# Rebalancing the first eleven slots of a top-k attention with a GELU layer behind it: normalisations to Pool, one addition and one copy later in their queues

## The chip, the cores and the metric

The kernel runs on one core of one Trainium2 chip. A core has five engines that each work through their own program in order and wait for each other by semaphores: TensorE (PE, with its weight loads shown apart as PEld), VectorE (DVE), ScalarE (ACT), GpSimd (Pool) and SyncE (SP), which here only issues transfers. The metric is the device time of one execution in microseconds. Before the change it is 1646.02 us, the median of three runs (1644.73 to 1646.81).

## The reference: what is computed

The inputs q, k and v are 8 batches x 8 heads x 576 rows x 64, and w_in (512 x 2048) and w_out (2048 x 512). For every row of scores the 32 largest are kept, and the softmax runs over them; then a two-layer block with the exact GELU follows.

```python
scores = scale * np.matmul(q, k.transpose(0, 1, 3, 2))
kth = np.partition(scores, -top_k, axis=-1)[..., -top_k:-top_k + 1]     # top_k = 32
scores = np.where(scores >= kth, scores, -1000000000.0)
scores = scores - np.max(scores, axis=-1, keepdims=True)
attn = np.exp(scores)
attn = attn / (np.sum(attn, axis=-1, keepdims=True) + 1e-09)
attn_out = np.matmul(attn, v)
x = attn_out.transpose(0, 2, 1, 3).reshape(B * S, H * D)                # 4608 x 512
h = x @ w_in
out = (0.5 * h * (1.0 + erf(h / sqrt(2)))) @ w_out
```

The two weights reach the kernel as 64-bit floats, seen as integers. The kernel turns them into 32-bit floats itself, with integer steps on their words: two ScalarE activations on the exponent part, a scaling of the low word ("conversion"), and two integer additions on Pool ("first sum" and "second sum").

## The kernel before

The work is cut into items: two heads of one batch by 128 rows of scores (the last 64 rows of two pairs of heads form one item). A loop over slots n keeps several items in flight: slot n computes the scores of item n+2, finds the 32 largest of item n (VectorE), runs the softmax of item n-1 (ScalarE), transposes the normalised item n-2 (TensorE, copied out of PSUM by ScalarE), multiplies a finished pair of items with v ("attend", item n-3), and fills TensorE with pieces of the two-layer block (`mlp`). The 16 units of the weights are converted in slots 1 to 15 and 17, one a slot. START is 10: the slot from which pieces of the two-layer block are there to do.

```python
def weights_size(u):                        # ScalarE, at the end of slot n-1 for the unit of slot n
    ...
    nc.scalar.activation(d, first, func=AF.Relu, bias=low, scale=2.0**19)
    nc.scalar.activation(below, first, func=AF.Prelu, bias=high, scale=2.0**-21, alpha=2.0**40)
    if not on_pool(u):                                                   # conversion, L179
        nc.scalar.activation(w.bitcast(i32), w.bitcast(u32), func=AF.Copy, scale=2.0**-13)

def on_pool(u):
    return SLOT_OF[u] >= START

def weights_add(u):                         # Pool, at the start of slot n
    if u in words:
        w, _, below, d = parts(u)
        if on_pool(u):                                                   # conversion, L191
            nc.gpsimd.tensor_scalar(w.bitcast(i32), w.bitcast(u32), 2.0**-13, None, op0=ALU.mult)
        nc.gpsimd.tensor_tensor(d, d, below, op=ALU.add)                 # first sum, L194
        nc.gpsimd.tensor_tensor(d, d, w.bitcast(i32), op=ALU.add)        # second sum, L195
    made.add(u)
...
def threshold(i):                           # Pool: neg (L345), bias (L348) for the softmax of item i
...
def inverse(i):                             # VectorE, L356
    nc.vector.reciprocal(st["rden"], st["den"])

def add_small(i):                           # Pool, L362
    nc.gpsimd.tensor_scalar(st["den"], st["den"], 1e-9, None, op0=ALU.add)

def softmax(i, e):                          # ScalarE, L369 and L370
    nc.scalar.activation(s, s, func=AF.Prelu, bias=st["neg"][:, e, 1:2], scale=1.0, alpha=STEEP)
    nc.scalar.activation(s, s, func=AF.Exp, bias=st["bias"][:, e : e + 1], scale=1.0,
                         accum_out=st["den"][:, e : e + 1])

def normalise(i, on_dve):                   # L382: on_dve of the two rows on VectorE, the others on Pool
    for e in range(2):
        s = row(i, e)
        (nc.vector if e >= 2 - on_dve else nc.gpsimd).tensor_scalar(
            s, s, st["rden"][:, e : e + 1], None, op0=ALU.mult)
...
# attend: 20 matmuls into o (L450), then
            nc.scalar.copy(out=xT[:, at, c], in_=o[:, 0:n])              # L455
...
# transposes: tails (matmul L401, copy L402), then main(0) and main(1) (matmuls L419, copies L426)
...
for n in range(ahead):
    left[0] = 4 if n in (START, START + 1) else 8
    eager[0] = n > N
    weights_add(unit_in(n))
    scores(n + 2)                           # matmuls L273, L277; copies L287, L288 on ScalarE
    product = attend(n - 3)
    late = n > START
    mlp(1)
    tr = transposes(n - 2)
    ...
    softmax(n - 1, 0)
    mlp(1)
    if not late:
        softmax(n - 1, 1)
    ...                                     # transposes of item n-2, pieces of q and k, mlp
    if late:
        softmax(n - 1, 1)
    add_small(n - 1)
    ...
    if n < N:
        top_k(n, {3: lambda: inverse(n - 1)})   # 8 maxima and 6 replacements on VectorE, then the reciprocal
    else:
        inverse(n - 1)
    threshold(n)
    u = unit_in(n + 1)
    normalise(n - 1, 0 if u not in words else 2 if on_pool(u) else 1)
    weights_size(unit_in(n + 1))
    if n >= FIRST:
        load_weights(n + 2)                 # into a staging place that the unit of slot n has left
```

tp_t, tp, t_ps, o and tp_qk share one pair of PSUM buffers.

Of the kernel before, what the change touches and what calls it, by code (L numbers as in the profile page):

```python
# [14 lines left out]
def kernel(  # L15
# [19 lines left out]
    nc = tc.nc  # L35
# [32 lines left out]
    xT = const.tile([P, KO, RING], f32, name="xT")  # L68
# [12 lines left out]
    def raw_of(n, pair):  # L81
        return raws[n][pair % len(raws[n])]

    def load(n, pair, queue=None, queue2=None):
        if pair >= n_pairs:
            return
        queue = queue or nc.sync
        queue2 = queue2 or queue
        b, h0 = pair // NP, 2 * (pair % NP)
        t, src = raw_of(n, pair), sources[n]  # L90
        for e in range(2):
            queue.dma_start(
                out=t[:, 0:NM, e, :], in_=src[b, h0 + e, 0:SM].rearrange("(t p) d -> p t d", p=P)
            )
            queue2.dma_start(out=t[e * TL : (e + 1) * TL, NM, e, :], in_=src[b, h0 + e, SM:S])
# [18 lines left out]
    def weights_of(u):  # L114

        if u < NWI:
            c, r = u // 2 * WS, u % 2 * 2
            return w_in, r, c, w_in_sb[:, r : r + 2, c : c + WS]
        r = 2 * (u - NWI)
        return w_out, r, 0, w_out_sb[:, r : r + 2, :]  # L120
# [4 lines left out]
    START = 2 * NP + 2  # L125
    WARM = 9
    words = {}
# [6 lines left out]
    SLOT_OF = {u: FIRST + i + (i == UNITS - 1) for i, u in enumerate(ORDER)}  # L134
    UNIT_IN = {n: u for u, n in SLOT_OF.items()}
    unit_in = UNIT_IN.get
# [29 lines left out]
    def parts(u):  # L166

        t, dst = words[u], weights_of(u)[3].bitcast(i32)
        return t[:, :, 0::2], t.bitcast(mybir.dt.int16)[:, :, 2::4], t[:, :, 1::2].bitcast(i32), dst
# [10 lines left out]

    def on_pool(u):

        return SLOT_OF[u] >= START

    made = set()

    def weights_add(u):
        if u in words:
            w, _, below, d = parts(u)
            if on_pool(u):  # L190
                nc.gpsimd.tensor_scalar(  # L191
                    w.bitcast(i32), w.bitcast(u32), 2.0**-13, None, op0=ALU.mult
                )
            nc.gpsimd.tensor_tensor(d, d, below, op=ALU.add)  # L194
            nc.gpsimd.tensor_tensor(d, d, w.bitcast(i32), op=ALU.add)  # L195
        made.add(u)


    items, starts = [], []
# [8 lines left out]
    def place_of(b, row):  # L208

        if row < SM:  # L210
            return b // 2 * RING + b % 2 * (SM + 2 * TL) + row
        return b // 2 * RING + SM + b % 2 * TL + row - SM
# [34 lines left out]
    def row(i, e):  # L247
        return S_of[i][:, e * S : (e + 1) * S]
# [5 lines left out]
    def half(r, e):  # L254


        return slice((r ^ e) * TL, ((r ^ e) + 1) * TL)
# [100 lines left out]
    def add_small(i):  # L358
        if i < 0 or i >= N:
            return  # L360
        st = stat_of[i]
        nc.gpsimd.tensor_scalar(st["den"], st["den"], 1e-9, None, op0=ALU.add)  # L362

    def softmax(i, e):

        if i < 0 or i >= N:
            return
        st, s = stat_of[i], row(i, e)
        nc.scalar.activation(s, s, func=AF.Prelu, bias=st["neg"][:, e, 1:2], scale=1.0, alpha=STEEP)  # L369
        nc.scalar.activation(  # L370
            s, s, func=AF.Exp, bias=st["bias"][:, e : e + 1], scale=1.0,
            accum_out=st["den"][:, e : e + 1],
        )

    def normalise(i, on_dve):

        if i < 0 or i >= N:
            return
        st = stat_of[i]
# [3 lines that stand above are left out]
                s, s, st["rden"][:, e : e + 1], None, op0=ALU.mult  # L383
            )
# [5 lines left out]
    def transposes(i):  # L390
# [24 lines left out]
        def main(e):  # L415
            tp = ps.tile([P, 512], f32, tag="tp", name="tp")
            first = e * (S + TL if t < NM else S)
            for j in range(NM):
                nc.tensor.transpose(  # L419
                    tp[:, j * P : (j + 1) * P], s[:, first + j * P : first + (j + 1) * P], ident  # L420
                )
            if t < NM:
                dst = pt_now[0][:, e * NM : (e + 1) * NM, t % 2 * P : (t % 2 + 1) * P]
            else:
                dst = ptt[:, e, 0:NM, :]
            nc.scalar.copy(out=dst, in_=tp.rearrange("p (j n) -> p j n", j=NM))  # L426

        return [tails] + [lambda e=e: main(e) for e in range(2)]

    n_tok, read = [0], [0]  # L430

    def attend(i):

        if i < 0 or i >= N:
            return False
        pair, t = items[i]
        b, at = divmod(pair, NP)
        if t < NM and t % 2 == 0:
            return False
        pt = pt_now[0]  # L440
        o = ps.tile([P, 512], f32, tag="tp", name="o")
        n, row = (2 * P, (t - 1) * P) if t < NM else (TL, SM)
        tok = place_of(b, row)
        assert read[0] >= tok + n - RING
        c = slice(tok % RING, tok % RING + n)
        if t < NM:
            vt = raw_of("v", pair)
            for j in range(NJ):
                for e in range(2):
                    nc.tensor.matmul(  # L450
                        o[e * D : (e + 1) * D, 0:n], lhsT=vt[:, j, e, :],
                        rhs=pt[:, e * NM + j if j < NM else 2 * NM, :],
                        start=(j == 0), stop=(j == NJ - 1),
                    )
            nc.scalar.copy(out=xT[:, at, c], in_=o[:, 0:n])  # L455
        else:
            for r in range(2):
                vt = raw_of("v", pair + r)
                for j in range(NJ):
                    for e in range(2):  # L460
                        nc.tensor.matmul(  # L461
                            o[e * D : (e + 1) * D, r * TL : (r + 1) * TL], lhsT=vt[:, j, e, :],
                            rhs=pt[:, r, j, half(r, e)], start=(j == 0), stop=(j == NJ - 1),
                        )
            nc.scalar.copy(
                out=xT[:, at : at + 2, c],
                in_=o[:, 0 : 2 * TL].rearrange("p (r n) -> p r n", r=2),
            )

        if t == (NM if b % 2 == 0 else NM - 1):  # L470
            for r in range(2 if t == NM else 1):
                load("v", pair + r + NP + 1)
        if at == (NP - 1 if t < NM else NP - 2):
            assert n_tok[0] == tok
            n_tok[0] = tok + n
        return True
# [111 lines left out]
    def mlp(n):  # L588
        for _ in range(n):
            if done[0] >= len(pieces) or pieces[done[0]][0] > ready[0] or left[0] == 0:  # L590
                return
            pieces[done[0]][1]()
            done[0] += 1
            left[0] -= 1
            if eager[0]:
                run_gelus()
# [38 lines left out]
# [5 lines that stand above are left out]
        scores(n + 2)  # L640
        product = attend(n - 3)
        late = n > START
        mlp(1)
        tr = transposes(n - 2)
        if product and n > START and done[0] < len(pieces) and pieces[done[0]][0] > ready[0]:

            for piece in tr[:1]:
                piece()
            tr, ready[0] = tr[1:], n_tok[0]
        softmax(n - 1, 0)  # L650
        mlp(1)
        if not late:
            softmax(n - 1, 1)
        mlp(1)
        prep = prep_in.pop(n, [])
        if len(prep) > 1 and len(tr) == 3:
            tr, prep = tr[:1] + prep[:1] + tr[1:], prep[1:]
        for piece in tr[:-1]:
            piece()
            ready[0] = n_tok[0]  # L660
            mlp(1)
        ready[0] = n_tok[0]
        if late:
            softmax(n - 1, 1)
        add_small(n - 1)
        for piece in tr[-1:] + prep:
            piece()
            mlp(1)

        run_gelus()  # L670
        mlp(left[0])
        run_gelus()
        if n < N:
            top_k(n, {3: lambda: inverse(n - 1)})
        else:
            inverse(n - 1)
        threshold(n)
        u = unit_in(n + 1)

        normalise(n - 1, 0 if u not in words else 2 if on_pool(u) else 1)  # L680

        weights_size(unit_in(n + 1))
        if n >= FIRST:
            load_weights(n + 2)
        if n <= NP:
            load("v", n)
# [38 lines left out]
```

## Time and profile before

The span of the profiled execution is 1643.7 us.

| engine | busy us | share of the span |
|---|---|---|
| TensorE, matmuls | 1589.8 | 97% |
| VectorE | 1421.2 | 86% |
| ScalarE | 1184.8 | 72% |
| Pool | 650.3 | 40% |

The operations that the change touches, with the mean time of one (in the first 150 us):

| line | engine | operation | ns |
|---|---|---|---|
| L382 | VectorE | normalisation, 128x576 | 520 |
| L382 | Pool | normalisation, 128x576 | 1729 |
| L194, L195 | Pool | first and second sum, 128x1024 | 2400, 2397 |
| L191 | Pool | conversion, 128x1024 | 3108 |
| L179 | ScalarE | conversion, 128x1024 | 1138 |
| L455 | ScalarE | copy to xT, 128x256 | 377 |

A page of the profile gives the busy time of each engine, a picture of the span in forty slices (about 41 us each, digits are tenths busy), and groups of instructions by line of the kernel. The trace behind it can be asked for the instructions of one engine in order of time, for who waited for whom, and for the busy time in chosen stretches. Times in these answers count from the start of the span. In a timeline a line reads: start, duration, engine, line, operation, output<-input, shape; the brackets hold the idle time of the engine just before it and what ended it. An average over the span mixes stages with different limits, so each stage has to be looked at by itself.

### The profile page before, as it was taken

How to read it: one execution, taken by the hardware profiler on the slowest of the kernel's cores; microseconds unless marked ns; L12 is line 12 of the kernel's file. 1: busy time of each engine (PE TensorE's matmuls, PEld its weight loads, DVE VectorE, ACT ScalarE, POOL GpSimd, SP SyncE). 2: the span in 40 equal slices, each digit the busy share in tenths (PEclk: the TensorE clock that was granted, in tenths of full speed). 3: DMA queues.
4: the chain of work that ended last, by engine and by line, in shares of the span. 5: the costliest groups of instructions: out<-in, count | busy, mean ns of one | idle time of the engine just before them, and what ended most of it. 6: DMA issues, size and time to landing. Idle time of an engine off the chain costs nothing.

```text
span 1643.7 us, 25039 instructions
## 1 busy us (share of the span) xinstructions
PE 1589.8 (97%) x8818; PEld 1076.9 (66%) x8818; DVE 1421.2 (86%) x3058; ACT 1184.8 (72%) x2131; POOL 650.3 (40%) x749
## 2 busy tenths in 40 slices
PE   6669999999999999999999999999999999999999
PEld 4346676766666666676666667676666666667665
DVE  7999999988899889998989888998889898999800
ACT  6889877777777777777777777777777777777620
POOL 3778633333333333333333333333333333333300
PEclk7779999999999999999999999999999999999999
DMA  6424210011101110011110111001110101000000
GB/s 179 141 86 132 55 43 1 14 29 43 37 1 29 30 34 24 1 28 36 29 28 9 34 30 43 1 14 29 44 36 1 28 16 35 2 14 1 7 13 13
DMA packets 126765, 56.14 MB, mean 34 GB/s; under 512 B 117776, under 2 KB 118064, under 8 KB 126640
## 3 DMA queue, kind: packets, MB, share of 16 engines
q1 hardware_dynamic: 125376, 54.12, 12.3%
q8 instruction: 70, 1.15, 0.3%
q14 instruction: 55, 0.45, 0.1%
q10 hardware_dynamic: 1200, 0.39, 0.1%
q0 software_dynamic: 64, 0.03, 0.0%
HBM read 45.08 MB, written 9.44 MB: 33 GB/s over the span
## 4 chain that ended last, share of the span: by engine, by line
PE 92%; DVE 6%; ACT 1%; POOL 1%; issue 0%; DVEq 0%; POOLq 0%; ACTq 0%
PE h_ps L502 31%; PE y_ps L538 30%; PE o L450 9%; PE s_ps L277 8%; PE tp L419 7%; DVE top L330 3%; DVE rest L333 2%; PE tp_qk L232 2%; PE t_ps L273 2%; PE o L461 1%; PE s_ps L304 1%; PE tp_t L401 1%; POOL s L382 1%; ACT s L370 0%; PE t_ps L293 0%; ACT s L369 0%
## 5 line engine op out<-in xcount | busy, mean ns | idle before, releaser
L330 DVE MAX8 top<-rest 128x8 f32<-128x576 f32 x864 | 609.2, 746 | 0.0
L502 PE MATMUL h_ps<-xT,w_in_sb 128*128 128x256 f32 (+1 forms) x2560 | 553.0, 361 | 0.0
L538 PE MATMUL y_ps<-w_out_sb,g 128*128 128x512 f32 x1152 | 548.9, 599 | 0.0
L502 PEld LDWEIGHTS h_ps<-xT,w_in_sb 128*128 128x128 f32 x2560 | 428.4, 191 | 61.8 <-issue 16.4
L382 POOL TENSOR_SCALAR s<-s,rden 128x576 f32<-128x576 f32 x266 | 456.6, 1727 | 0.4 <-DVE rden L356 0.4
L333 DVE MATCH_REPLACE8 rest<-top,rest 128x576 f32<-128x576 f32 x576 | 423.2, 742 | 0.0
L362 POOL TENSOR_SCALAR den<-den 128x2 f32<-128x2 f32 x144 | 32.1, 223 | 831.4 <-ACT s L370 830.9
L538 PEld LDWEIGHTS y_ps<-w_out_sb,g 128*128 128x128 f32 x1152 | 195.1, 190 | 168.2 <-issue 167.3
L287 ACT ACTIVATE s<-s_ps 128x1024 f32<-128x1024 f32 x127 | 130.6, 1028 | 164.6 <-PE s_ps L277 142.2
L370 ACT ACTIVATE s<-s,bias 128x576 f32<-128x576 f32 x288 | 223.4, 776 | 13.2 <-ACT s L369 0.7
L369 ACT ACTIVATE s<-s,neg 128x576 f32<-128x576 f32 x288 | 224.1, 778 | 0.3 <-POOL neg L345 0.2
L426 ACT COPY pt<-tp 128x512 f32<-128x512 f32 x256 | 147.3, 575 | 102.8 <-PE tp L419 102.7
L419 PEld LDWEIGHTS tp<-ident,s 128*128 128x128 f32 x1152 | 145.7, 144 | 113.9 <-issue 58.4
L333 DVE MATCH_REPLACE8 rest<-top,s 128x576 f32<-128x576 f32 x288 | 211.6, 742 | 0.0
L419 PE MATMUL tp<-ident,s 128*128 128x128 f32 x1152 | 178.4, 279 | 26.8 <-ACT pt L402 20.7
L330 DVE MAX8 top<-s 128x8 f32<-128x576 f32 x288 | 201.8, 742 | 1.4 <-ACT s L283 1.4
L450 PE MATMUL o<-pt,raw_v 128*64 128x256 f32 x1280 | 156.8, 392 | 0.0
L277 PE MATMUL s_ps<-qk 64*128 64x256 f32 x1024 | 151.7, 416 | 0.8 <-ACT s L285 0.8
L356 DVE RECIPROCAL rden<-den 128x2 f32<-128x2 f32 x144 | 23.0, 160 | 136.1 <-POOL den L362 135.8
L450 PEld LDWEIGHTS o<-pt,raw_v 128*64 128x64 f32 x1280 | 88.3, 140 | 67.1 <-issue 24.2
L277 PEld LDWEIGHTS s_ps<-qk 64*128 64x128 f32 x1024 | 91.6, 193 | 23.6 <-issue 1.6
L513 ACT ACTIVATE g<-h_ps 128x512 f32<-128x512 f32 x144 | 78.6, 595 | 37.8 <-PE h_ps L502 37.1
(71 smaller groups left out, 1087.2 us busy)
## 6 DMA issues: line engine op xcount, KB each, us to landing
raw_q<-in_q_dram SPq DMA_DIRECT2D x64, 128.0 KB, 2.4
raw_v<-in_v_dram SPq DMA_DIRECT2D x64, 128.0 KB, 2.5
w_out_sb<-in_moe_w_in_dram SPq DMA_DIRECT2D x16, 511.8 KB, 4.7
raw_k<-in_k_dram SPq DMA_DIRECT2D x62, 128.0 KB, 2.5
out_dram<-y SPq DMA_DIRECT2D x31, 256.0 KB, 2.2
w_out_sb<-in_moe_w_out_dram SPq DMA_DIRECT2D x10, 511.8 KB, 4.2
words<-in_moe_w_out_dram SPq DMA_DIRECT2D x6, 511.8 KB, 4.6
out_dram<-y SPq DMA_DIRECT2D x9, 128.0 KB, 2.3
```

Of the source, the lines that this page charges most:

```text
L277: nc.tensor.matmul(s_ps[:, e, c * 256 : (c + 1) * 256], lhsT=lhsT[rows, :], rhs=qk[rows, KT + c * 256 : KT + (c + 1) * 256], start=True, s ...
L287: nc.scalar.activation(spread(s, S + TL, SM), s_ps, func=AF.Copy, scale=scale)
L330: nc.vector.max(st["top"][:, e, 8 * r : 8 * r + 8], cur[e])
L333: nc.vector.match_replace(rest[:, e], st["top"][:, e, 8 * r : 8 * r + 8], cur[e], LOWEST)
L369: nc.scalar.activation(s, s, func=AF.Prelu, bias=st["neg"][:, e, 1:2], scale=1.0, alpha=STEEP)
L370: nc.scalar.activation(s, s, func=AF.Exp, bias=st["bias"][:, e : e + 1], scale=1.0, accum_out=st["den"][:, e : e + 1],)
L382: (nc.vector if e >= 2 - on_dve else nc.gpsimd).tensor_scalar(s, s, st["rden"][:, e : e + 1], None, op0=ALU.mult)
L419: nc.tensor.transpose(tp[:, j * P : (j + 1) * P], s[:, first + j * P : first + (j + 1) * P], ident)
L426: nc.scalar.copy(out=dst, in_=tp.rearrange("p (j n) -> p j n", j=NM))
L450: nc.tensor.matmul(o[e * D : (e + 1) * D, 0:n], lhsT=vt[:, j, e, :], rhs=pt[:, e * NM + j if j < NM else 2 * NM, :], start=(j == 0), stop= ...
L502: nc.tensor.matmul(h_tile(u)[:, i, :], lhsT=w_in_sb[:, ko, f * P : (f + 1) * P], rhs=xT[:, ko, c0 : c0 + n], start=(ko == 0), stop=(ko == ...
L538: nc.tensor.matmul(y_of[sub], lhsT=g_of[u][:, i, sub * P : (sub + 1) * P], rhs=w_out_sb[:, f, :], start=(f == 0), stop=(f == FT - 1),)
```

## The change

Four things change, all in slots up to 11.

- Normalisations: where the next slot's unit lies in slots 2 to 11, both rows are now normalised on Pool. Before, one of two was on VectorE up to slot 8, and both in slots 9 and 10. From slot 11 on nothing changes here.
- The conversion (the scaling of the low word) of the units of slots 10 and 11 goes from Pool to ScalarE.
- Up to slot 10 Pool does the second sum of the weights behind the small addition to the softmax's denominator and no longer ahead of it. From slot 11 the two sums stay together.
- Up to slot 10 ScalarE's copy of attention's result to xT stands behind the first softmax and no longer ahead of it.

It is meant to spread the work of the first slots differently over VectorE, Pool and ScalarE, and to let ScalarE do a softmax while TensorE is still at attention.

```diff
     def on_pool(u):
-        return SLOT_OF[u] >= START
+        return u in words and SLOT_OF[u] >= START + 2
 ...
             nc.gpsimd.tensor_tensor(d, d, below, op=ALU.add)
+            if not ends_late(u):
+                weights_end(u)
+        made.add(u)
+
+    def ends_late(u):
+        return u in words and SLOT_OF[u] <= START
+
+    def weights_end(u):
+        if u in words:
+            w, _, _, d = parts(u)
             nc.gpsimd.tensor_tensor(d, d, w.bitcast(i32), op=ALU.add)
-        made.add(u)
 ...
+    def copy_x():
+        while copies:
+            copies.pop()()
 ...
-            nc.scalar.copy(out=xT[:, at, c], in_=o[:, 0:n])
+            copies.append(lambda: nc.scalar.copy(out=xT[:, at, c], in_=o[:, 0:n]))
 ...
         product = attend(n - 3)
         late = n > START
+        if n <= START:
+            softmax(n - 1, 0)
+        copy_x()
         mlp(1)
         tr = transposes(n - 2)
 ...
-        softmax(n - 1, 0)
+        if n > START:
+            softmax(n - 1, 0)
         mlp(1)
 ...
         add_small(n - 1)
+        if ends_late(unit_in(n)):
+            weights_end(unit_in(n))
 ...
-        normalise(n - 1, 0 if u not in words else 2 if on_pool(u) else 1)
+        normalise(n - 1, 2 if on_pool(u) else 0)
```

More of the change, by code (lines that the diff above doesn't have):

```diff
@@ L428, in transposes @@
         return [tails] + [lambda e=e: main(e) for e in range(2)]
+    def copy_x():
+        while copies:
+            copies.pop()()
     n_tok, read = [0], [0]
+    copies = []
     def attend(i):
@@ L464, in attend @@
                         )
-            nc.scalar.copy(
+            copies.append(lambda: nc.scalar.copy(
                 out=xT[:, at : at + 2, c],
                 in_=o[:, 0 : 2 * TL].rearrange("p (r n) -> p r n", r=2),
-            )
+            ))
         if t == (NM if b % 2 == 0 else NM - 1):
```

## The prediction, made before the changed kernel ran

> **What bounds the kernel now.** I read the page first: shares of the engines and the forty slices.
>
> ```profile
> PE 1589.8 (97%) x8818; PEld 1076.9 (66%) x8818; DVE 1421.2 (86%) x3058; ACT 1184.8 (72%) x2131; POOL 650.3 (40%) x749
> ...
> PE   6669999999999999999999999999999999999999
> DVE  7999999988899889998989888998889898999800
> ...
> PEclk7779999999999999999999999999999999999999
> ```
>
> TensorE is busy for 97% of the span, and what it lacks lies in the first three slices (about 120 us). The change touches only slots up to 11, which are just those. So the question is not what the change saves in busy time, but how much earlier TensorE comes into its unbroken stretch. The busy time by stretches says when that begins:
>
> ```profile
> core 0: us, PE busy (x) PEld busy (x) DVE busy (x) ACT busy (x) POOL busy (x), PEclk, DMA share, GB/s
> ...
> 61.00:112.00 51.00, 28.05 (x141) 18.47 (x141) 50.61 (x110) 45.78 (x76) 36.27 (x30) 0.74 0.33 106
> 112.00:133.00 21.00, 17.94 (x102) 12.96 (x101) 20.79 (x46) 16.85 (x29) 17.42 (x12) 0.90 0.37 118
> 133.00:187.00 54.00, 54.00 (x301) 35.04 (x301) 52.11 (x113) 48.92 (x81) 38.98 (x28) 0.97 0.31 100
> ```
>
> From 133 us TensorE has no gap (1324.0 of 1324 us busy from 206 to 1530 us, too). From 61 to 112 us VectorE is full (50.61 of 51) and looks like the bound. But the list of waits up to 150 us has no wait of ScalarE for VectorE; ScalarE waits for TensorE, and TensorE for ScalarE:
>
> ```profile
> PE tp L419 <- ACT pt L402: 20.7, 9, 2.7
> ...
> ACT xT L455 <- PE o L450: 5.0, 3, 2.1
> ...
> PE t_ps L273 <- ACT pt L426: 1.6, 2, 1.4
> ```
>
> The columns are total us, times and longest. (The third line is from 112 to 210 us.) ScalarE's own timeline shows it with hardly a gap from 30 us on, except where it copies attention's result to xT:
>
> ```profile
> 56.18 0.37 ACT L455 COPY xT<-o 128x256 f32<-128x256 f32 x1 [1.87 <-PE o L450]
> ...
> 76.41 0.37 ACT L455 COPY xT<-o 128x256 f32<-128x256 f32 x1 [1.04 <-PE o L450]
> ...
> 95.53 0.41 ACT L455 COPY xT<-o 128x256 f32<-128x256 f32 x1
> ...
> 117.76 0.37 ACT L455 COPY xT<-o 128x256 f32<-128x256 f32 x1 [2.07 <-PE o L450]
> ```
>
> I number slots by the threshold on Pool that ends each: slot 1 at 30.3 us, slot 9 at 112.6. ScalarE begins slot n at the copy of the scores (L287): 31.88 us in slot 2, 114.50 in slot 10, so 10.33 us a slot. VectorE's slot, from reciprocal to reciprocal, is 10.27 us (30.09 to 40.37). Both run at the same rate; but the softmax of slot 9 begins 3.3 us after its threshold (106.28 against 102.95), so VectorE is ahead, and **ScalarE with TensorE sets the pace**. At 132.57 us TensorE begins slot 12 after a wait for ScalarE's L426, and from there it is the bound.
>
> **What the Trainium skill says.** "Perfetto Trace Analysis", section Optimization Strategy: where the busiest engine changes over time, take each regime by itself and look for the gaps there. This trace has such regimes, as above. "GPSIMD Engine Reference", section 4.1, prefers VectorE for elementwise work, with one-input work on GpSimd roughly at line rate; here a normalisation of 128x576 takes 1.73 us on Pool and 0.52 on VectorE, 3.3 times as long. "ScalarE: Activation LUTs", section What ACT_TABLE_LOAD costs, lets back-to-back ACTIVATEs overlap by about 93 ns; the trace agrees: L179 lasts 1.14 us at 104.20, and the next starts 1.02 later. "TensorE: Matmul & The Clock Gate", section What's actually happening: the clock is throttled by default, and activity releases it. The granted clock here is 0.60 from 30 to 61 us, 0.74, 0.90, then 0.97; the same 20 matmuls of attention take 3.4 us at 134.7 and 2.3 at 157.6.
>
> **The change, part by part.**
>
> *1. Normalisations.* In slots 1 to 8 one of two leaves VectorE, in slots 9 and 10 both. The first costs VectorE's slot 10.27 - 9.83 = 0.44 us (9.66 for the top-k of slot 0, from 10.79 to 20.45, plus 0.17 for the reciprocal's step), the two together 0.94 (10.77 against 9.83). That is 8 x 0.44 + 2 x 0.94 = 5.4 us off VectorE by the end of slot 10. It isn't on the path, so worth nothing by itself; it keeps VectorE's lead when ScalarE becomes faster, which it must: without it VectorE would go on at 10.27 and eat the 3.3 us.
>
> *2. Pool's load.* In slots 1 to 8, from start to start: threshold 0.31 + 0.26, one normalisation 1.70, two additions 2.48 + 2.49, the small addition 0.22: 7.5 us. After: 9.2, within VectorE's 9.83. In slots 10 and 11 the conversion (L191, 3.12 us) goes to ScalarE and two normalisations come: 3.4 for 3.2, no change.
>
> *3. Second sum behind the small addition.* den is ready about 7 us after the preceding reciprocal (99.25 against 91.78). The first sum then ends at 0.17 + 0.57 + 3.40 + 2.48 = 6.6 after it; with both sums ahead, the small addition would come at 9.1, and VectorE would come close to waiting. Behind it, the second sum runs from about 7.3 to 9.8, and the threshold can be up to 1 us late. The softmax has some 3 us of slack there. So this part is what makes part 1 bearable, and gains nothing more.
>
> *4. The copy to xT behind the first softmax.* Four copies lie in slots up to 10. A softmax of 128x576 takes 0.87 + 0.78 = 1.65 us and with its step some 1.7; it fills the wait up to that. Slot 4: 1.7 of 1.87. Slot 6: 1.04, all. Slot 8: no wait. Slot 10: all that is left of 2.07, some 1.7. On ScalarE's path: **1.7 + 1.0 + 1.7 = 4.4 us**. The transposes behind them need the PSUM buffer that the copy frees, 1.6 us later than now relative to the scores, but ScalarE takes their results only after the second softmax, so nothing waits.
>
> *5. Conversions of slots 10 and 11 to ScalarE.* Two L179 of 1.03 us (step): **+2.1 us**. The first lies at the end of slot 9, the second at the end of slot 10.
>
> *The sum on the path.* ScalarE reaches L402 of slot 9 2.7 us earlier (106.8). TensorE begins slot 10 at 108.9 for 111.6 and ends attention at 115.0 for 117.7. ScalarE starts slot 10 after the added conversion at 112.4, copies xT at 115.2 without a wait, is at L402 at 117.1 for 121.25. TensorE's last transposes of slot 10 come at 117.9 for 121.55: 3.65 earlier. Then ScalarE has the second added conversion: L287 of slot 11 at 123.8 for 126.44 (2.6 earlier), but the 0.51 us for which L426 now waits in slot 11 goes into it: second L426 done at 129.3 for 132.5. So **TensorE enters slot 12 about 3.2 us earlier**. Normalised rows for slot 11 are on Pool until 123.9, and TensorE wants them at 124.7: just in time. From slot 12 on the programs are the same: the gain should stand to the end. 1646.0 - 3.2 = 1642.8. If TensorE waits less there, its clock may rise sooner: the attention at 134.7 would lose up to 1.1 us, taken at a fifth. I say **1642.6**.
>
> **The rivals.** (a) *Pool becomes the bound in slots 2 to 11.* For it: 9.2 of 9.83 us, with a wait for den in the middle. If every slot lost 0.5 us, ten would cost 5 us, and the time would be about 1647. Against: the closed chain den, small addition, second sum, threshold, softmax, den is only 0.3 + 2.5 + 0.6 + 3.3 = 6.7 us. TensorE does wait for Pool's normalised rows already (6.7 us in five slots, at tp_t), but ScalarE comes to that transpose only some 5 us later (65.6 is when it starts the softmax that stands ahead of it, the wait ended at 63.4). (b) *The added conversions eat everything*, as the waits they fill aren't those that the copy frees: gain 0 to 1 us, 1645 to 1646. For it: slots 9 and 10 are where ScalarE is tightest. (c) *VectorE is the real bound*, and 5.4 us come through: 1640.5. Against: no wait for it in the list up to 133 us. (d) *Weights arrive later*, as the staging buffer is free only after the second sum, now up to 3 us later. The load for slot 7 is issued at 68.6 and lands 4.6 us after (median), wanted at 81.4: it stays hidden.
>
> **Range and chances.** The sum has two terms of about 4.4 and 2.1 us, each uncertain by a third, and the clock for another 1 us; the three times of before spread over 2.1 us. I take **1639.2 to 1645.6**. A move of 2% is 33 us, while all of the first 133 us can't shrink by that: faster 0.01, within 2% 0.98, slower 0.01.
>
> **What would show it.** VectorE's reciprocals 9.8 us apart in slots 2 to 9. Waits of the xT copy for attention gone, or below 0.3 us. Two more L179 on ScalarE, two L191 fewer on Pool (3.1 us each). TensorE's entry to slot 12 near 129.3 us for 132.57; the unbroken stretch behind it of equal length, and the end earlier by the same. It is wrong if TensorE waits at tp_t for Pool's normalisation for more than a microsecond a slot, if VectorE waits for den before slot 11, or if the gain at slot 12 is there but lost by 206 us, where TensorE now waits 0.7 us for Pool.

## The result, and the profile after

The changed kernel takes **1640.70 us** (median of 6 runs, 1640.09 to 1642.20) against 1645.57 before (6 runs): ratio 0.9971, interval 0.9958 to 0.9984. The gain is clear of the measurement's noise and is 4.9 us by the medians; 3.4 us were forecast, with a range of 1639.2 to 1645.6.

The page of the changed kernel, shares of the engines and the forty slices:

```profile
PE 1589.1 (97%) x8818; PEld 1077.1 (66%) x8818; DVE 1415.4 (86%) x3046; ACT 1185.5 (72%) x2133; POOL 662.3 (40%) x759
...
PE   6669999999999999999999999999999999999999
...
PEclk7679999999999999999999999999999999999999
```

At this coarseness almost nothing is to be seen. VectorE has lost 5.8 us of busy time and Pool has gained 12; TensorE looks the same. The stretches show the difference (same columns as before the change):

```profile
61.00:112.00 51.00, 28.35 (x145) 19.02 (x143) 50.84 (x112) 46.78 (x76) 46.16 (x39) 0.73 0.33 110
112.00:133.00 21.00, 18.96 (x118) 13.54 (x118) 18.80 (x41) 19.71 (x34) 19.21 (x15) 0.94 0.55 176
133.00:187.00 54.00, 53.22 (x300) 35.38 (x297) 49.87 (x107) 48.30 (x82) 36.52 (x27) 1.00 0.27 81
```

Pool works 46.16 of 51 us where it worked 36.27. From 112 to 133 us TensorE is busy for 18.96 us where it was for 17.94: its unbroken stretch starts sooner. The moment to read is its entry to slot 12, the first matmuls of scores after its wait for ScalarE's copy. TensorE's timeline, the changed kernel first, then the kernel before:

```profile
129.92 0.49 PE L283 MATMUL t_ps<-qk 128*128 128x128 f32 x2 [1.39 <-ACT pt L436]
```

```profile
132.57 0.49 PE L273 MATMUL t_ps<-qk 128*128 128x128 f32 x2 [1.39 <-ACT pt L426]
```

From there to the end of the span it is 1640.4 - 129.9 = 1510.5 us after the change, and 1643.7 - 132.6 = 1511.1 before. **All of the gain is in that one moment, but for 0.6 us.** Those 0.6 come from the clock: attention in slot 12 (20 matmuls) took 3.44 us before and takes 2.38 here. The profiled run of the changed kernel was one of its slower ones (1642.19 us), so its trace shows 3.3 of the 4.9 us.

ScalarE's copies to xT, whose waits were to be filled, in its timeline after:

```profile
57.32 0.37 ACT L471 COPY xT<-o 128x256 f32<-128x256 f32 x1 [0.84 <-PE o L466]
...
76.50 0.35 ACT L471 COPY xT<-o 128x256 f32<-128x256 f32 x1
...
95.62 0.35 ACT L471 COPY xT<-o 128x256 f32<-128x256 f32 x1
...
116.29 0.35 ACT L471 COPY xT<-o 128x256 f32<-128x256 f32 x1
```

Of 5.0 us in three waits 0.84 are left, in one.

### The profile page after: what moved, and what is told of

Read it like the earlier page. It is cut to its first block, busy times and chain, and to the rows that moved or that the text cites. A ratio compares the mean times of both kernels' runs of the same rounds, so it can differ in the third digit from the quotient of the medians.

```text
span 1640.4 us, 25030 instructions
## 1 busy us (share of the span) xinstructions
PE 1589.1 (97%) x8818; PEld 1077.1 (66%) x8818; DVE 1415.4 (86%) x3046; ACT 1185.5 (72%) x2133; POOL 662.3 (40%) x759
## 4 chain that ended last, share of the span: by engine, by line
PE 92%; ACT 5%; issue 1%; DMA 1%; DVE 1%; POOL 0%; SPq 0%; ACTq 0%; DVEq 0%; POOLq 0%
PE y_ps L554 30%; PE h_ps L518 30%; PE o L466 9%; PE tp L429 8%; PE s_ps L287 8%; PE tp_qk L242 2%; PE t_ps L283 2%; PE o L477 1%; ACT s L380 1%; PE s_ps L314 1%; ACT s L379 1%; PE tp_t L411 1%; ACT s L297 1%; ACT w_out_sb L179 1%; ACT w_in_sb L175 1%
## 5 line engine op out<-in xcount | busy, mean ns | idle before, releaser
L392 POOL TENSOR_SCALAR s<-s,rden 128x576 f32<-128x576 f32 x278 | 476.5, 1723 | 0.6 <-DVE rden L366 0.4
L297 ACT ACTIVATE s<-s_ps 128x1024 f32<-128x1024 f32 x127 | 130.4, 1027 | 165.7 <-PE s_ps L287 143.8
L436 ACT COPY pt<-tp 128x512 f32<-128x512 f32 x256 | 147.1, 574 | 102.2 <-PE tp L429 102.2
```

The lines of the kernel that those rows point to most:

```text
L297: nc.scalar.activation(spread(s, S + TL, SM), s_ps, func=AF.Copy, scale=scale)
```

## The experiments

Theory A: ScalarE and TensorE, waiting for each other, set the pace up to slot 11, and the gain is the copy's filled waits. Theory B: VectorE's relief is the gain. Each time below is a median beside runs of the kernel before on the same chip.

**The copy alone**, on the kernel before:

```diff
-            nc.scalar.copy(out=xT[:, at, c], in_=o[:, 0:n])
+            copies.append(lambda: nc.scalar.copy(out=xT[:, at, c], in_=o[:, 0:n]))
 ...
+        if n <= START:
+            softmax(n - 1, 0)
+        copy_x()
```

> The kernel before with part 4 alone: the copy to xT behind the first softmax up to slot 10; normalisations, sums and conversions as before. Theory A (ScalarE and TensorE set the pace, the copy's waits are the gain): about 4 us faster than before (4.4 us of waits filled, no added conversion), 1641 to 1642, with VectorE's lead of 3.3 us nearly used up by slot 10. Theory B (VectorE's relief is the gain): as before, 1645 to 1646. TensorE's entry to slot 12 (132.6 us before, 129.9 with the whole change): A near 129, B near 132.5.

Measured: 1641.64 us for 1645.40, ratio 0.9977 (0.9969 to 0.9985); TensorE enters slot 12 at 129.20. As theory A had it.

**All but the copy**: the changed kernel with `copy_x()` ahead of `softmax(n - 1, 0)` again.

> The changed kernel with part 4 undone: the copy to xT ahead of the first softmax again, all else as changed. Theory A: no gain, rather a loss of up to 1 us against before from the conversions added to ScalarE, 1645.5 to 1647. Theory B: about 5 us faster than before all the same, near 1641.

Measured: 1646.43 us, ratio 1.0006 (0.9998 to 1.0014). The other parts without the copy bring nothing; whether they cost something is not resolved.

**The sums together**: `ends_late` always false, so that the second sum stands ahead of the small addition in all slots.

> The changed kernel with the second sum ahead of the small addition in all slots. If the order on Pool matters as part 3 had it (den ready at about 7 us after the reciprocal, both sums only at 9.1): VectorE waits for den now and then, up to 0.3 us a slot, and the time is 0 to 1 us above the changed kernel, 1640.7 to 1641.7. Rival: the small addition stands on the path, and each slot loses a large part of the 2.4 us sum: 1645 or more.

Measured: 1640.39 us, ratio 0.9972 (0.9961 to 0.9984), as with the whole change. VectorE waits once, 0.8 us, for the small addition up to 133 us. The order on Pool is worth nothing that these runs resolve.

**VectorE filled**: idle multiplications where its normalisations stood.

```diff
         normalise(n - 1, 2 if on_pool(u) else 0)
+        if 1 <= n <= START and u in words and not on_pool(u):
+            for _ in range(1 if n < START - 1 else 2):
+                nc.vector.tensor_scalar(idle_row, idle_row, stat_of[n - 1]["rden"][:, 0:1], None, op0=ALU.mult)
```

> The changed kernel with idle multiplications of 128x576 on VectorE where the normalisations stood (one in slots 1 to 8, two in slots 9 and 10), beside those that Pool does now. VectorE's slot is back at 10.3 us. Theory A: its lead of 3 us takes up most of it, 0 to 1.5 us above the changed kernel, 1641 to 1642. Theory B: all of the gain is lost, near 1645.6.

Measured: 1645.06 us, ratio 0.9998 (0.9989 to 1.0006). The whole gain is gone, where theory A allowed a loss of 1.5 us at most. The list of waits from 30 to 133 us, this kernel and then the changed one:

```profile
PE tp_t L413 <- POOL s L392: 31.2, 9, 6.7
```

```profile
PE tp_t L411 <- POOL s L392: 14.6, 5, 4.8
```

VectorE's reciprocal comes 10.3 us after the last one again, and Pool's two rows come late: in slot 10 they are ready 4.5 us after the reciprocal (127.76 for 123.27). With the copy alone, on VectorE, it is 1.2 us (124.15 for 122.94). In slot 11 TensorE is ready for them and waits; its timeline, this kernel and then the copy alone:

```profile
127.81 0.33 PE L413 MATMUL tp_t<-ident,s 128*128 128x128 f32 x1 [1.67 <-POOL s L392]
```

```profile
124.91 0.27 PE L401 MATMUL tp_t<-ident,s 128*128 128x128 f32 x1
```

Followed back from TensorE's entry to slot 12 (132.16 us), the chain of this kernel runs through that transpose to Pool's two rows, and from there, from 123.4 us back to 60, through VectorE alone: in this kernel VectorE is the bound. So VectorE's relief and Pool's slower rows go together: the one pays for the other, and theory A as I had it lacked that price. Theory B's number came true here, but VectorE's relief by itself brings nothing, as a later run shows.

**Slots 10 and 11 as before**: `on_pool` from START on, in the changed kernel; conversions back on Pool, both normalisations of slots 9 and 10 on VectorE.

> The changed kernel with slots 10 and 11 as before: their conversions on Pool again, and with them both normalisations of slots 9 and 10 on VectorE. If the two conversions cost ScalarE 2.1 us on the path (part 5), TensorE enters slot 12 about 1.5 to 2 us earlier than in the changed kernel (129.9 us there) and the time is 1639 to 1640. Rival: the conversions lie in waits, or VectorE's longer slots 9 and 10 cost as much: 1640.5 to 1641.5.

Measured: 1640.93 us, ratio 0.9969 (0.9959 to 0.9980), as with the whole change: the rival. The 2.1 us of part 5 don't come back. Whether they lie in waits, or are paid for by VectorE's longer slots 9 and 10, this run doesn't tell.

**TensorE kept busy**: idle matmuls on zeros in its waits of slots 1 to 9.

```diff
+        for x, piece in enumerate(tr[:-1]):
+            if n < START:
+                keep_warm((0 if product else 12, 3 if product else 0)[min(x, 1)])
             piece()
+            if n < START and x == len(tr) - 2:
+                keep_warm(4)
```

> The changed kernel with idle matmuls on zeros in TensorE's waits of slots 1 to 9 (12 of them ahead of the first transposes, or 3 behind an attention, and 4 between the last two groups), so that its clock does not fall. The granted clock from 61 to 112 us should rise from 0.73 towards 1. Theory A: ScalarE's waits for the last transposes shrink from 0.72 to 0.26 us a slot, 2 to 3 us in all, 1638 to 1639. Rival: the pace is held by VectorE or by buffers, and nothing moves, 1640.7, or the idle matmuls delay the real ones and it is slower.

Measured: 1641.34 us, ratio 0.9975 (0.9966 to 0.9985), no better than the changed kernel. The clock did rise; the same stretch of this kernel:

```profile
61.00:112.00 51.00, 40.89 (x273) 30.60 (x272) 51.00 (x112) 48.01 (x77) 45.92 (x37) 0.87 0.35 117
```

0.87 for 0.73. Yet ScalarE's waits for the last transposes went only from 5.4 to 4.0 us in all. The changed kernel's line:

```profile
ACT pt L436 <- PE tp L429: 5.4, 10, 0.7
```

Six of these ten waits were of 0.72 us, and four of 0.26 already. With the idle matmuls three are still of 0.7: behind two of them the four transposes still took 1.11 us, for 0.66 where the clock was up, and the third stands behind transposes that idle matmuls held up. And ScalarE has a new wait, for a weight transfer, as long as most of what was won (whether the idle matmuls brought it about is not shown):

```profile
59.67 1.27 ACT L175 ACTIVATE w_out_sb<-w_out_sb,low 128x1024 int32<-128x1024 int16 x1 [0.99 <-DMA w_out_sb<-in_moe_w_out_dram]
```

A miss.

**The tails' copy ahead of the second softmax**, on the changed kernel, up to slot 10:

```diff
         if not late:
+            if len(tr) == 3:
+                tr[0]()
+                tr[0] = lambda: None
             softmax(n - 1, 1)
```

> The changed kernel with the copy of the transposed tails (L412) ahead of the second softmax up to slot 10: TensorE's last transposes wait for that copy's buffer and would run beside the second softmax, so that ScalarE's wait of 0.72 us a slot goes. Theory A: up to 0.7 us a slot, as far as VectorE's slot of 9.7 us allows it; TensorE enters slot 12 some 2 us earlier, 1638 to 1639.5. Rival: ScalarE then waits at the tails for Pool's normalisation instead, 1640.7 or slower.

Measured: **1638.28 us**, ratio 0.9956 (0.9944 to 0.9969). TensorE enters slot 12 at 125.87. ScalarE's waits for the last transposes, 5.4 us in ten with the changed kernel, are 0.7 in one:

```profile
ACT pt L436 <- PE tp L429: 0.7, 1, 0.7
```

**The same step with the copy to xT, on the kernel before**, so with VectorE at 10.3 us a slot:

> The kernel before with the copy to xT moved (as in the run with the copy alone) and also the copy of the tails ahead of the second softmax; normalisations, sums and conversions as before, so VectorE's slot is 10.3 us. In the run with the copy alone the softmax of slot 11 began only 0.4 us after its threshold, so VectorE's lead is gone. If so, a faster ScalarE brings nothing: 1641 to 1642, as with the copy alone, while the same step on the changed kernel gains. Rival (VectorE still has slack): 2 us faster than with the copy alone.

Measured: 1641.55 us, ratio 0.9975 (0.9965 to 0.9986), as with the copy alone. Here the waits have a line that neither the kernel before nor the changed one has:

```profile
ACT s L369 <- POOL neg L345: 2.4, 3, 1.3
```

The softmax waits for the threshold, which Pool writes as soon as VectorE's top-k is done. **VectorE has become the bound.** ScalarE can be made no faster without it.

**Two more on the version with the tails' copy (1638.28 us)**: with the sums together, and with slots 10 and 11 as before.

> The version with the tails' copy ahead of the second softmax (1638.3 us), and the second sum ahead of the small addition again in all slots. On the changed kernel that order made no difference. If Pool's 9.2 us still fit into VectorE's slot of 9.7 us, it makes none here either: 1638 to 1638.8. Rival: with ScalarE faster, den is ready before both sums are done, VectorE waits for the small addition, and the time rises by over 1 us, 1639.3 or more.

Measured: 1638.26 us, ratio 0.9956 (0.9943 to 0.9970). No difference.

> The version with the tails' copy ahead of the second softmax (1638.3 us), with slots 10 and 11 as before the change: conversions on Pool, both normalisations of slots 9 and 10 on VectorE. If VectorE is now as tight as ScalarE, its longer slots 9 and 10 (1.1 us each) cost what the two conversions free: 1638 to 1639. Rival: ScalarE still sets the pace there, and the 2.1 us of the conversions come through: 1636 to 1637.3.

Measured: 1637.96 us, ratio 0.9953 (0.9941 to 0.9966). Not told apart from 1638.28.

**One step of part 1 by itself**: both normalisations of slots 1 to 8 on Pool, first on the kernel before, then on the kernel before with both of ScalarE's copies moved.

```diff
-        normalise(n - 1, 0 if u not in words else 2 if on_pool(u) else 1)
+        normalise(n - 1, 2 if u in words and on_pool(u) else 0)
```

> The kernel before with one step of part 1 alone: in slots 1 to 8 both normalisations on Pool (slots 9 and 10, conversions, sums and copies as before). VectorE is 8 x 0.57 = 4.6 us shorter. Theory A (ScalarE with TensorE sets the pace in the kernel before): no gain, 1645 to 1646.5. Theory B: 3 to 4.6 us faster, 1641 to 1642.5.

Measured: 1645.64 us, ratio 0.9998 (0.9990 to 1.0006). No gain.

> The same step on the kernel before with both of ScalarE's copies moved (1641.55 us, where ScalarE waited for VectorE's threshold). If VectorE was the bound there, the same step that alone brings nothing now brings about 3 us: 1638 to 1638.5, and the order of the sums and the place of the conversions add nothing. Rival (those other parts are needed too): 1640 or more.

Measured: **1637.13 us**, ratio 0.9946 (0.9932 to 0.9959), the lowest median of all these kernels, though its interval overlaps those of the versions at 1638 us. It has neither the second sum moved nor the conversions on ScalarE.

| | rows of slots 1 to 8 shared with VectorE | rows on Pool |
|---|---|---|
| ScalarE's copies as before | 1645.86 us | 1645.64 us |
| both copies moved | 1641.55 us (ratio 0.9975) | 1637.13 us (ratio 0.9946) |

One line of code is worth nothing in the upper row and some 4 us in the lower.

## Why the prediction was right, point by point

- **What bounds the kernel before: right.** The copy alone gives 1641.64 us, VectorE's relief alone (slots 1 to 8) nothing. What the other parts add to the copy is not resolved: ratio 0.9977 (0.9969 to 0.9985) for the copy alone, 0.9971 (0.9958 to 0.9984) for the whole change. TensorE's unbroken stretch is of nearly the same length in all these traces (1510.5 us, or 1511.1 to 1511.2 where the matmuls at its start ran cold and in the kernel before with both copies moved), so its entry to slot 12 decides.
- **The copy's waits: right in the sum, not slot by slot.** Forecast 4.4 us of 5.0; the trace shows 4.2 filled: 1.03 in slot 4 for a forecast 1.7, 1.04 in slot 6, and all 2.07 in slot 10 for 1.7. Slot 4 kept 0.84 us because its attention, begun at the same point of ScalarE's slot as before, took 4.11 us for 3.49; the granted clock over it was 0.56 for 0.67.
- **The entry to slot 12: right, in part by luck.** Forecast 129.3, measured 129.92. In this trace ScalarE began slot 2 at 32.45 us for 31.88 before, 0.57 later, which goes back to its copy of item 1's scores at 18.00 for 17.13: the first slots, in front of what the change touches. With 0.57 taken off, the last steps agree to 0.1 us: L297 of slot 11 at 124.36 for a forecast 123.8, second L436 done at 129.86 for 129.3. But those between still come some 0.5 us late (L412 of slot 9 at 107.95 for 106.8, of slot 10 at 118.12 for 117.1), as slot 4 filled less. It is made up in slot 10: TensorE's last transposes came 0.3 us after that L412 (118.42), where I had put 0.8. And 3.2 us on the path is what this trace shows, not every run (see below the list).
- **The clock: undersized.** I gave the warm attention of slot 12 a fifth of 1.1 us. It came whole (2.38 us for 3.44), and the scores ahead of it took 1.13 us for 1.71; of that 0.78 went into a new wait for ScalarE's L412 at 139.6 us. Net 0.6.
- **VectorE's relief: undersized.** Its slot is 9.70 us (reciprocals at 29.96 and 39.66) for a forecast 9.83. One normalisation is worth 0.57 us a slot, not 0.44.
- **Part 3, the step that failed.** I held that the second sum's place makes part 1 bearable. The sums together cost nothing, here or with a faster ScalarE, since Pool's 9.2 us fit into 9.7 either way. In the changed kernel VectorE even waits more for den (2.7 us in four waits up to 133 us) than with the sums together (0.8 in one). And the second sum holds up the threshold by more than the 1 us that I allowed: in slot 4 it begins 2.4 us after the reciprocal (62.04 for 59.61), for 0.2 in the kernel before, and Pool's rows follow it.
- **Part 5: too dear on the path, or balanced.** Undoing it moves no median. Its two terms, conversions off ScalarE and two rows on VectorE, were undone together, so their single sizes stay open.
- **The rivals.** Pool did not become the bound in the changed kernel: TensorE's waits at tp_t rose to 14.6 us, yet ScalarE came later still. But the margin was thinner than I said: with VectorE 0.6 us a slot slower, the chain through VectorE and Pool's rows took the whole gain. Rival (c), VectorE, stands right behind ScalarE: on the kernel before, with both copies moved, it takes over.
- **Weights arriving later: hidden**, as forecast; no such transfer is among ScalarE's waits in the changed kernel.
- **The signs of being wrong: two of three came true.** VectorE waited for den before slot 11 (1.0 us of the first line below), and TensorE waited at tp_t for Pool's rows by more than 1 us a slot: 14.6 us in five of the slots 2 to 11. The second line comes on top; it is put down to a transfer, but the wait ended at 35.12 us, just as Pool's rows were done (35.07).

```profile
DVE rden L366 <- POOL den L372: 2.7, 4, 1.7
PE tp_t L411 <- DMA w_out_sb<-in_moe_w_in_dram: 3.1, 1, 3.1
```

The gain stands all the same: ScalarE waited for neither, as its waits from 30 to 133 us are all for TensorE's matmuls. As signs these were badly chosen; a wait tells against the forecast only if it lies on the path.

Why do the medians differ by 4.9 us and these traces by 3.3? The profiled run took 1.5 us more than the median. The trace of the sums together (1640.39 us), a kernel that takes the same time by its median, shows more of the gain: there attention in slot 4 took 2.79 us at a granted clock of 0.84, no copy to xT waited, and TensorE entered slot 12 at 128.12, 4.4 us earlier than before. So TensorE's clock in slot 4 made some of the difference between these two traces; whether it does so between other runs is not shown. Runs of the changed kernel spread over 2.1 us, those of the kernel before with both copies moved, with VectorE as the bound, over 0.7 (1641.16 to 1641.86).

## What to carry to other kernels

Where two engines ran at the same rate, taking work off one was worth nothing until the other had lost its waits; so test a step again after the next one, and test parts of a change by themselves. The engine that is full (VectorE, 50.6 of 51 us) need not be the one that sets the pace: look for who waits for it. And in a program whose last part is one unbroken stretch of one engine, read a change by when that stretch begins: one line of a timeline told more than any share of busy time.

## What the runs showed of the hardware

Pool and VectorE slowed each other a little where their multiplications of 128x576 overlapped. In slots 9 and 10 of the kernel with VectorE filled, VectorE's two idle multiplications still ran for 0.5 us when Pool's two normalisations had begun, and these took 3.74 us both times; in the changed kernel, beside VectorE's top-k, they took 3.43. VectorE's two took 1.09 us, for 0.95 in the kernel before. Pool's conversion, begun there 0.3 us before the end of such a pair, was not slowed (3.08 and 3.12 us, mean 3.11). Timelines, VectorE filled and then the changed kernel:

```profile
112.61 1.09 DVE L708 TENSOR_SCALAR ptt<-ptt,rden 128x576 f32<-128x576 f32 x2
...
113.17 3.74 POOL L392 TENSOR_SCALAR s<-s,rden 128x576 f32<-128x576 f32 x2
```

```profile
111.30 3.43 POOL L392 TENSOR_SCALAR s<-s,rden 128x576 f32<-128x576 f32 x2
```

The Trainium skill, "GPSIMD Engine Reference", section 8 (Key points), has GpSimd share its SBUF interfaces with VectorE, with contention where VectorE's instruction is in a two-port mode or has two SBUF inputs. The slower multiplications agree with that, if VectorE's ran in such a mode, which no run here shows.
